# Gated linear attention with a diagonal state-space branch on one core: banks and order in the passage between two loops, kv ahead of q in three chunks, tiles moved by 64 bytes

## The chip, the cores and the metric

The kernel runs on one core of a Trainium2 chip. The metric is device time in microseconds (us) of one execution, the median of several. The core has five engines with queues of their own, each working in program order: TensorE (PE; its weight loads are listed as PEld), VectorE (DVE), ScalarE (ACT), GpSimd (POOL) and SyncE (SP), which here only issues DMA transfers. All times below are from one profiled execution unless a median is named.

## The reference

For x of 2048 rows and D = 448 columns, H = 16 heads of 28:

```python
phi = lambda t: jnp.where(t > 0, t + 1, jnp.exp(t)) + 1e-6
pq, pk = phi(q), phi(k)                      # q, k, v = x @ wqkv
kv = jnp.einsum("bhsd,bhse->bhde", pk, v)
z = jnp.einsum("bhsd->bhd", pk)
num = jnp.einsum("bhqd,bhde->bhqe", pq, kv)
den = jnp.einsum("bhqd,bhd->bhq", pq, z)[..., None] + 1e-6
a = (num / den) @ wo
b = causal_conv(x, K(log_A_real, A_imag, C_real, C_imag, log_dt)) + x * D_skip
out = g * a + (1 - g) * b                    # g = sigmoid((x * gate_w).sum(-1))
```

Nothing is causal in branch a: kv and z are sums over all rows, so every output row needs all of pk first. In branch b the convolution kernel is, for these inputs, so flat that running sums of x do its work: a triangular matrix (tri) times the chunk, a factor per column (near), and a carry from earlier chunks (the product z).

## The kernel before

The sequence is cut into NC = 16 chunks of 128 rows. Nearly all matmuls are in fp32r, and each factor is split into a high and a low part, so that a product takes two or three matmuls: ACT writes the high part (a cast), POOL or DVE the low part (the difference).

**Chunk loop** (lines 464 to 517; chunk c does k of chunk c + 1 and the rest of chunk c). On PE: k, 11 matmuls of 448 columns (project, lines 309 to 332); q, 11 of 450 columns; kv, 11 matmuls g (do_g, line 386), where pkh and pkl, the high and low part of pk, stream against blocks of x and add up in four PSUM banks over all chunks; and from chunk 5 on one or two products v with tri (do_v, line 399; two matmuls, lines 401 and 402). What feeds them: split_t (line 232) casts x turned into xt on ACT and has POOL write its low half, for k and q of that chunk; the second matmul of a k already needs the low half. split_n (line 237) does the same for x as it is, xn, for kv and v, and has POOL do skip (line 245). k_feature, k_high and k_low (lines 348 to 363) make pkh and pkl on ACT and DVE; q_post (line 370) starts on ACT with an exp of q's last column (line 371). v_post (line 404) multiplies v on DVE (line 406), sends a row by SP, and has POOL add (line 414). In chunks below 5, steps() puts pieces of the state-space preparation on ACT and DVE behind q_post.

**Passage** (lines 627 to 771). When all kv sums stand, ACT copies them out (gs), and PE makes, in this order: z, the carry product of branch b (line 681: uw, whose 47 rows hold the chunk's last rows of v at rows 0 to 14 and their low parts at rows 32 to 46); kv_products(1) into a tile called k, for heads of blocks 2 and 3, and kv_products(0) into a tile called tr (line 712; 16 pieces each). kv_split (line 715) masks them on DVE, kv_high and kv_low write kvh (ACT) and kvl (DVE). m_products (line 688) multiply those by the split wo, three matmuls for each block j = 3, 2, 0, 1, into m3, m2, m0, m1; m_high (ACT) and m_low (DVE, line 700) write them to mh and ml, the operands of the output products. Block 3 goes to a tile shl, whose low part is needed before SP copies pieces of it to other rows (lines 751 and 752). Tiles that share a PSUM bank with an earlier one wait until that is read: m3 takes the bank of the tile k, m2 that of z, m0 and m1 take two free ones of the pool p3.

Meanwhile the denominators are made per chunk: norm_a (POOL, prod = pq times z's sums, line 527; three buffers), norm_b (DVE, a reduction, line 532), norm_d (DVE, scale and reciprocal, and a copy to SBUF by DVE or ACT, lines 535 to 541), norm_c (pq divided, pn: two instructions on POOL and one on DVE, lines 547 to 560).

**Output loop** (lines 796 to 821). Chunk by chunk: turn (four transposes of pn on PE, line 589; ACT casts th, DVE writes the low part, line 597), attend (11 matmuls, line 614, in the order of blocks 2, 0, 1, 3), final_b and final_c. turn(c + 1) stands ahead of attend(c) on PE. The seven remaining matmuls of the last q are put into the passage (q_run).

The order is that of the code: nothing is scheduled by a tool. Tile addresses follow from the order in which tiles are allocated; the short tile edge (64 bytes) shifts all pools behind it.

Of the kernel before, what the change touches and what calls it, by code (L numbers as in the profile page):

```python
# [7 lines left out]
F32 = mybir.dt.float32  # L8
F32R = mybir.dt.float32r
# [6 lines left out]
P = 128  # L16
S = 2048
D = 448
# [3 lines left out]
NC = S // P  # L22
# [20 lines left out]
GIN = 9 + NC  # L43
L1, L0 = 32, 64
UL = 32
UZ = UL + NC - 1
PAD = S + P
MAGIC = 1.5 * 2.0 ** 23
TWO_PI = 6.283185307179586
# [85 lines left out]
def gated_mix_kernel(ctx: ExitStack, tc: tile.TileContext, xin, wq_d, wvo_d, abc_d, ldt_d, dsk_d,  # L135
# [19 lines left out]
    wqh, wql = (const.tile([P, J, QW], F32R, name=n)[:, :, :D + 2] for n in ("wqh", "wql"))  # L155
    wvo = const.tile([P, 2, J, D], F32, name="wvo")
    wv, wo = wvo[:, 0], wvo[:DJ, 1]
    tri = const.tile([P, P], F32R, name="tri")
    both = const.tile([P, 2, P], F32, name="both")
    ident, trir = both[:, 0], both[:, 1]  # L160
    cst = const.tile([P, DJ + RX + 1], F32, name="cst")
# [10 lines left out]
    okr = const.tile([1, DJ + 1], F32, name="okr")  # L172

    const.tile([P, EDGE], F32, name="edge")

    xp = work.enter_context(tc.tile_pool(name="xp", bufs=4))
    xt_p = work.enter_context(tc.tile_pool(name="xt", bufs=4))
# [59 lines left out]
    def split_n(c):  # L237
        r, w = plain[c], xn_p.tile([P, NX], F32R, name="xn", tag="n")
        xn[c] = w
        ACT.copy(w[:, :XC - NAT], r)  # L240
        low(POOL, w[:, XC - NAT:], r[:, :D], w[:, :D])
        if c > 2:
            skip(c)
# [85 lines left out]
    def project(*args, **kw):  # L329
        o, run = pieces(*args, **kw)  # L330
        run(11)
        return o
# [20 lines left out]
        DVE.scalar_tensor_tensor(out=pks[c], in0=pks[c], scalar=1.0, in1=e, op0=ALU.add, op1=ALU.max)  # L353

    def k_high(c):
        pkh[c] = tp.tile([P, D], F32R, name="pkh", tag="pkh")
        ACT.add(pkh[c], pks[c], 1e-6)

    def k_low(c):
        pk = pks.pop(c)  # L360
        pkl[c] = tp.tile([P, D], F32R, name="pkl", tag="pkl")
        for o, a, op in ((pkl[c], pkh[c].bitcast(F32), ALU.subtract), (zb, zb, ALU.add))[::-1 if c == NC - 1 else 1]:
            DVE.scalar_tensor_tensor(out=o, in0=pk, scalar=1e-6, in1=a, op0=ALU.add, op1=op)

# [5 lines left out]
    def q_post(c, o, mid=None):  # L370
        ACT.activation(e1[:, c:c + 1], o[:, D:D + 1], AF.Exp, scale=-1.0)
        feature(pq[:, c], o, mid)
# [13 lines left out]
    def do_g(c, blocks=range(4)):  # L386
        w = xn[c]
        for i in blocks:
            a = w[:, 64 + i * P:64 + (i + 1) * P]
            b = w[:, XC - NAT + 64 + i * P:][:, :P] if i < 3 else None  # L390
            seq = [(a, pkh[c]), (a, pkl[c]), (b, pkh[c])] if i < 3 else \
                  [(a, pkh[c]), (a[:, :64], pkl[c])][::1 if c == 0 else -1]
            for n, (a, b) in enumerate(seq):
                PE.matmul(g[i][:a.shape[1], :D], lhsT=a, rhs=b, start=c == 0 and n == 0,  # L394
                          stop=c == NC - 1 and n == len(seq) - 1)
# [68 lines left out]
    for c in range(2, NC - 2):  # L464
        if c + 3 < NC:
            load_x(c + 3)
        if c == 2:
            SP.dma_start(out=cst, in_=cst_d)
        if c == 4:
            SP.dma_start(out=wvo, in_=wvo_d)  # L470
        vs = VS.get(c, ())
        ko = project(c + 1, wkh, wkl, D, "v1" if c in (2, 4) else "k")
        for v in vs[:1]:
            do_v(v)
        split_t(c + 2)
        k_feature(c + 1, ko)
        k_high(c + 1)
        if c > 5:
            for v in vs[:1]:
                v_post(v)  # L480
        k_low(c + 1)
        qo = project(c, wqh, wql, D + 2, "q")
        if c == 5:
            steps(1)
        else:
            for v in vs[1:]:
                do_v(v)
        q_post(c, qo)
        if c == 5:
            v_post(0)  # L490
        else:
            for v in vs[1:]:
                v_post(v)
        if c < 5:
            steps(2 if c == 4 else 1)
        if c == 3:
            DVE.tensor_copy(tri, trir)
            DVE.tensor_copy(gcr, gcat)
        if c == 7:
            SP.dma_start(out=okr[:, None, :DJ], in_=oks[:, None, :])  # L500
        if c == 9:
            DVE.tensor_reduce(out=okr[:, DJ:], in_=okr[:, :DJ], op=ALU.add, axis=AX.X)
            DVE.tensor_copy(okn, okr[:, DJ:])
        do_g(c)
        if c == 5:
            do_v(1)
        if c < 4:
            skip(c - 1)
        split_n(c + 2)
        if c == 5:  # L510
            v_post(1)
        for j in {11: (0, 1), 12: (2, 3)}.get(c, ()):
            w = xn_p.tile([P, NX], F32R, name="wo", tag="n")[:DJ, :2 * D].rearrange("p (i d) -> p i d", i=2)
            woh.append(w[:, 0])
            wol.append(w[:, 1])
            ACT.copy(woh[j], wo[:, j])
            low(POOL, wol[j], wo[:, j], woh[j])
# [7 lines left out]
    def norm_a(c):  # L525
        pd[c] = tp.tile([P, D], F32, name="prod", tag="pk", bufs=3)
        POOL.tensor_tensor(out=pd[c], in0=pq[:, c], in1=zb, op=ALU.mult)  # L527
# [15 lines left out]
    def norm_bd(c):  # L543
        norm_b(c)
        norm_d(c, 1)

    def norm_c(c):
        n = pn[c] = tp.tile([P, J, P], F32, name="pn", tag="pn")
        r = dn[c // 2][:, c % 2]
        a = pq[:, c, :3 * DJ].rearrange("p (j h d) -> p j h d", j=3, h=4)  # L550
        b = pq[:, c, 3 * DJ:].rearrange("p (h d) -> p h d", h=4)
        POOL.tensor_tensor(out=n[:, :3, :DJ].rearrange("p j (h d) -> p j h d", h=4), in0=a,  # L552
                           in1=r[:, :H - 4].rearrange("p (j h) -> p j h", j=3)[:, :, :, None].to_broadcast([P, 3, 4, DH]),
                           op=ALU.mult)
        DVE.tensor_tensor(out=n[:, :3, DJ:].rearrange("p j (h d) -> p h j d", h=4),  # L555
                          in0=b[:, :, :DS].rearrange("p h (j d) -> p h j d", j=3),
                          in1=dp[0][:, c, H - 4:, None, None].to_broadcast([P, 4, 3, DS // 3]), op=ALU.mult)
        POOL.tensor_tensor(out=n[:, 3].rearrange("p (b h d) -> p b h d", b=2, h=4),
                          in0=b[:, None, :, DS:].to_broadcast([P, 2, 4, DH - DS]),
                          in1=r[:, None, H - 4:, None].to_broadcast([P, 2, 4, DH - DS]), op=ALU.mult)  # L560
# [15 lines left out]
    def gates_c(n, o, tag):  # L576
        w = tp.tile([P, D], F32R, name="phs", tag=tag)[:n, :3 * P].rearrange("p (i t) -> p i t", i=3)
        phs.append(w)
        ACT.copy(w[:, 0:2], o[:n, None, :P].to_broadcast([n, 2, P]))
        return lambda: DVE.tensor_tensor(out=w[:, 2], in0=o[:n, :P], in1=w[:, 0].bitcast(F32), op=ALU.subtract)  # L580
# [77 lines left out]
    for i in range(4):  # L658
# [4 lines left out]
            q_run(2)  # L663
        if i == 2:
            gates_b(gates_a(1, NC - 1), g[0])
    gates_c(NC - 2, g[0], "pkl")()
    norm_bd(1)
    norm_c(1)
    for i in range(5):
        phi(i)  # L670
    gps.close()
# [16 lines left out]
    def m_products(j, pool, tag):  # L688
        o = pool.tile([P, 512], F32, name="m%d" % j, tag=tag)
        w = woh[j]  # L690
        for n, (a, b) in enumerate(((kvh, w), (kvh, wol[j]), (kvl, w))):
            PE.matmul(o[:DJ, :D], lhsT=a[:, j], rhs=b, start=n == 0, stop=n == 2)  # L692
        return o
# [34 lines left out]
    def kv_high(r, o):  # L728
        ACT.copy(kvh[:, 2 * r:2 * r + 2], o)

    def kv_low(r, o):
        DVE.tensor_tensor(out=kvl[:, 2 * r:2 * r + 2], in0=o, in1=kvh[:, 2 * r:2 * r + 2].bitcast(F32), op=ALU.subtract)
# [3 lines left out]
    k0 = kv_products(0)  # L736
    k1 = kv_split(1, k1)
    kv_high(1, k1)
    norm_a(3)
    kv_low(1, k1)  # L740
    k0 = kv_split(0, k0)
    carry()
    o3 = m_products(3, ps, "k")
    o2 = m_products(2, ps, "v0")
    m_high(3, o3)
    kv_high(0, k0)
    m_low(3, o3)
    kv_low(0, k0)
    m_high(2, o2)
    for j in (2, 0, 1):  # L750
        SP.dma_start(out=wk2[DJ:, :, j].bitcast(F32), in_=shl[DT + 16 * j:DT + 16 * j + 16].bitcast(F32))
# [3 lines left out]
    q_run(2)  # L755
    norm_a(4)
    turn_split(0, o0)
    o0 = m_products(0, p3, "a")
    o1 = m_products(1, p3, "a")
    m_high(0, o0)  # L760
    m_high(1, o1)
    m_low(0, o0)
    m_low(1, o1)
    ACT.copy(mh[:DT, 3], shl[:DT, 0].bitcast(F32))
    ACT.copy(rc[0][:DT], shl[:DT, 0].bitcast(F32))
    norm_bd(2)
    norm_c(2)
    norm_a(5)
    norm_bd(3)
    tail(0)  # L770
    q_run(11)
    def late():
# [21 lines left out]
    later = late()  # L794
    due = next(later)
    for c in range(NC):
        if c % 2 and c + 4 < NC:
            norm_d(c + 3, 2, ACT.copy)
        if c:
            final_b(c - 1)  # L800
        if 0 < c < NC - 2:
            norm_c(c + 2)
        if c + 1 < NC:
            turn(c + 1)
        if c:
            final_c(c - 1)
        if c + 1 < NC:
            tail(c + 1)
        if c + 6 < NC:
            norm_a(c + 6)  # L810
        if c + 5 < NC - 1:
            phi(c + 5)
        attend(c, ((0, D // 2), (D // 2, D)) if c == NC - 1 else ((0, D),))
        if c == 0:
            norm_b(4)
        if c + 5 < NC:
            norm_b(c + 5)
        if c == due:
            due = next(later, None)
        if c == 9:  # L820
            v_add(NC - 1, vl)
# [94 lines left out]
```

## Time and profile before

| | us |
|---|---|
| median of 3 executions | 177.37 (177.36 to 177.40) |
| the profiled execution | 177.07 |
| its span, first to last instruction | 175.3 |
| PE busy in the span | 169.2 |
| granted TensorE clock | 1.00 throughout |

Rows of the timeline give the start in us from the start of the span, the time taken, the engine, the line, the operation, what is written from what, the shape and how many instructions the row merges; in square brackets the engine's idle time before it and what ended it. A matmul's end is modelled and overlaps the next one, so the distance from start to start is its cost. PE's stages: start-up to about 8, chunk loop to 118.8, passage to about 129, output loop to 171.7.

### The profile page before, as it was taken

What the parts mean: (1) busy time and instruction counts of PE and PEld (TensorE: products, weight loads), DVE (VectorE), ACT (ScalarE), POOL (GpSimd) and SP (SyncE); (2) the same over time, 40 slices, a digit from 0 to 9 for tenths busy, and PEclk for the clock granted to TensorE, in tenths of its full rate; (3) what the DMA queues carried; (4) which work ended last, traced back from release to release, by engine and by line L of the source; (5) the groups of instructions that cost most, each with busy time, mean ns of one, the idle gap of its engine ahead of it and who ended that gap; (6) DMA issues with size and microseconds to landing.
All of it is one profiled execution on the core that took longest, in us unless ns stands there. A gap on an engine that the chain in (4) does not pass through costs nothing.

```text
span 175.3 us, 2809 instructions
## 1 busy us (share of the span) xinstructions
PE 169.2 (97%) x876; PEld 151.6 (86%) x876; DVE 114.1 (65%) x244; ACT 95.9 (55%) x220; POOL 120.5 (69%) x128
## 2 busy tenths in 40 slices
PE   6999999999999999999999999999899999999991
PEld 2698999999999999999989999988797999999991
DVE  1757548698867383563824519377899988987451
ACT  3789398884446344272435653464554554664541
POOL 5267576977349969687698999439549998983100
PEclk9999999999999999999999999999999999999999
DMA  5999974095003113031133000000021212122312
GB/s 174 415 301 300 245 212 142 23 410 226 4 1 121 58 65 119 7 121 52 69 122 121 4 0 1 0 2 4 14 54 52 105 69 93 75 101 88 112 57 104
DMA packets 7963, 18.61 MB, mean 106 GB/s; under 512 B 2045, under 2 KB 4810, under 8 KB 7818
## 3 DMA queue, kind: packets, MB, share of 16 engines
q1 hardware_dynamic: 7946, 18.41, 31.6%
q8 instruction: 7, 0.11, 0.3%
q14 instruction: 10, 0.08, 0.2%
HBM read 14.38 MB, written 3.67 MB: 103 GB/s over the span
## 4 chain that ended last, share of the span: by engine, by line
PE 85%; DVE 8%; ACT 2%; issue 2%; POOL 1%; ACTq 0%; DVEq 0%; POOLq 0%
PE g L394 19%; PE a L614 18%; PE q L325 17%; PE k L325 14%; PE v L325 6%; PE tr L589 4%; PE q L252 2%; PE v L402 2%; DVE den L532 2%; PE v L401 2%; PE m L692 1%; DVE wk L700 1%; DVE den L538 1%; POOL xn L230 1%; ACT gs L660 1%
## 5 line engine op out<-in xcount | busy, mean ns | idle before, releaser
L614 PE MATMUL a<-wk,th 128*128 128x448 f32 (+1 forms) x170 | 36.6, 360 | 0.0
L394 PE MATMUL g<-pkh,xn 128*128 128x448 f32 x112 | 35.8, 366 | 0.0
L614 PEld LDWEIGHTS a<-wk,th 128*128 128x128 f32 x170 | 29.5, 189 | 2.0 <-DVE th L597 0.4
L325 PE MATMUL k<-wk,xt 128*128 128x448 f32 x132 | 29.3, 366 | 0.0
L353 DVE SCALAR_TENSOR_TENSOR k<-k,e 128x448 f32<-128x448 f32 x12 | 7.6, 632 | 30.7 <-ACT e L352 30.7
L325 PE MATMUL q<-wqh,xt 128*128 128x450 f32 x120 | 27.4, 365 | 0.0
L325 PEld LDWEIGHTS k<-wk,xt 128*128 128x128 f32 x132 | 24.6, 188 | 2.8 <-ACT wk L423 0.4
L414 POOL TENSOR_TENSOR y<-y,t 128x448 f32<-128x448 f32 x16 | 18.7, 1167 | 11.9 <-DVE t L406 11.8
L230 POOL TENSOR_TENSOR xn<-xr,xn 128x448 fp32r<-128x448 f32 x16 | 19.2, 1203 | 9.1 <-ACT xn L240 8.8
L325 PEld LDWEIGHTS q<-wqh,xt 128*128 128x128 f32 x120 | 22.5, 188 | 1.7
L394 PE MATMUL g<-pkl,xn 128*128 128x448 f32 x64 | 23.5, 367 | 0.0
L394 PEld LDWEIGHTS g<-pkh,xn 128*128 128x128 f32 x112 | 21.1, 188 | 2.4
L351 ACT ACTIVATE e<-k 128x448 f32<-128x448 f32 x12 | 6.5, 543 | 27.5 <-PE k L325 27.4
L527 POOL TENSOR_TENSOR prod<-pq,zb 128x448 f32<-128x448 f32 x16 | 18.2, 1147 | 3.0 <-ACT zb L650 3.0
L246 POOL TENSOR_TENSOR y<-xr,rows 128x448 f32<-128x448 f32 x16 | 18.8, 1176 | 0.0
L230 POOL TENSOR_TENSOR xt<-xr,xt 128x512 fp32r<-128x512 f32 x14 | 18.1, 1296 | 0.4 <-ACT xt L234 0.4
L552 POOL TENSOR_TENSOR pn<-pq,den 128x336 f32<-128x336 f32 x16 | 12.0, 751 | 9.3 <-DVE pn L555 4.4
L619 DVE SCALAR_TENSOR_TENSOR ot<-y,og,a 128x448 f32<-128x448 f32 (+1 forms) x17 | 10.6, 626 | 5.1 <-PE a L614 5.0
L597 DVE TENSOR_TENSOR th<-tr,th 128x512 fp32r<-128x512 f32 x16 | 11.0, 690 | 2.8 <-ACT th L596 2.2
L394 PEld LDWEIGHTS g<-pkl,xn 128*128 128x128 f32 x64 | 11.2, 175 | 1.1
L596 ACT CAST th<-tr 128x512 fp32r<-128x512 f32 x16 | 9.4, 589 | 4.6 <-PE tr L589 4.4
L325 PE MATMUL q<-wql,xt 128*128 128x450 f32 x45 | 11.7, 364 | 0.0
(151 smaller groups left out, 301.9 us busy)
## 6 DMA issues: line engine op xcount, KB each, us to landing
xr<-in SPq DMA_DIRECT2D x15, 512.0 KB, 5.8
out<-ot SPq DMA_DIRECT2D x15, 224.0 KB, 1.9
pq<-in SPq DMA_DIRECT2D x4, 448.0 KB
wvo<-in SPq DMA_DIRECT2D x1, 1792.0 KB
y<-in SPq DMA_DIRECT2D x2, 480.0 KB
y<-in SPq DMA_DIRECT2D x2, 450.0 KB
u<-t SPq DMA_DIRECT2D x30, 1.8 KB, 1.8
y<-in SPq DMA_DIRECT2D x1, 448.0 KB, 4.3
```

The source lines that it names most:

```text
L230: eng.tensor_tensor(out=o, in0=r, in1=h.bitcast(F32), op=ALU.subtract)
L246: POOL.tensor_tensor(out=y[:, c], in0=plain[c][:, :D], in1=dsk, op=ALU.mult)
L325: PE.matmul(o[:, :n], lhsT=a, rhs=b, start=run.n == 1, stop=not seq)
L353: DVE.scalar_tensor_tensor(out=pks[c], in0=pks[c], scalar=1.0, in1=e, op0=ALU.add, op1=ALU.max)
L394: PE.matmul(g[i][:a.shape[1], :D], lhsT=a, rhs=b, start=c == 0 and n == 0, stop=c == NC - 1 and n == len(seq) - 1)
L414: POOL.tensor_tensor(out=y[:, c], in0=y[:, c], in1=t, op=ALU.add)
L527: POOL.tensor_tensor(out=pd[c], in0=pq[:, c], in1=zb, op=ALU.mult)
L552: POOL.tensor_tensor(out=n[:, :3, :DJ].rearrange("p j (h d) -> p j h d", h=4), in0=a, in1=r[:, :H - 4].rearrange("p (j h) -> p j h", j=3)[ ...
L596: ACT.copy(h, ov)
L597: DVE.tensor_tensor(out=l, in0=ov, in1=h.bitcast(F32), op=ALU.subtract)
L614: PE.matmul(a[:, lo:hi], lhsT=u_, rhs=w_[:, lo:hi], start=n == 0, stop=n == 10)
L619: DVE.scalar_tensor_tensor(out=ot[:, lo:hi], in0=y[:, c, lo:hi], scalar=og[:, c:c + 1], in1=a[:, lo:hi], op0=ALU.mult, op1=ALU.add)
```

## The change

Six edits; line numbers grow by up to 12.

1. In chunks 2 to 4 kv (do_g) is issued ahead of q, elsewhere behind it as before. On PE, from k of chunk 3 on (here called v_321 after its bank; g_141 to g_144 are the four kv banks), before:

```order
L325 MATMUL v_321<-wk_69,xt 128x448 x11
L325 MATMUL q<-wqh,xt 128x450 x8
L325 MATMUL q<-wql,xt 128x450 x3
L394 MATMUL g_141<-pkh,xn 128x448
L394 MATMUL g_141<-pkl,xn 128x448
```

and the end of that kv in the changed kernel:

```order
L394 MATMUL g_144<-pkl,xn 64x448
L394 MATMUL g_144<-pkh,xn 128x448
L325 MATMUL q<-wqh,xt 128x450 x8
L325 MATMUL q<-wql,xt 128x450 x3
L325 MATMUL k<-wk_69,xt 128x448 x11
```

The 11 kv matmuls now stand between k and q, and the next k follows q directly. The other engines' order in these chunks is unchanged, so q's work on ACT and DVE stands where it stood.

2. In chunk 10, split_n(12) is issued before the second v_post. On POOL, before (xt, xn and the two kinds of y are the low halves, skip at line 246 and the addition at line 414):

```order
L230 TENSOR_TENSOR xt<-xr,xt 128x512
L414 TENSOR_TENSOR y<-y,t 128x448 x2
L230 TENSOR_TENSOR xn<-xr,xn 128x448
L246 TENSOR_TENSOR y<-xr,rows 128x448
L230 TENSOR_TENSOR xt<-xr,xt 128x512
```

and in the changed kernel:

```order
L230 TENSOR_TENSOR xt<-xr,xt 128x512
L414 TENSOR_TENSOR y<-y,t 128x448
L230 TENSOR_TENSOR xn<-xr,xn 128x448
L246 TENSOR_TENSOR y<-xr,rows 128x448
L414 TENSOR_TENSOR y<-y,t 128x448
L230 TENSOR_TENSOR xt<-xr,xt 128x512
```

The second addition has moved behind xn and skip.

3. In the passage, norm_b(1) is issued ahead of the gates (line 580), norm_c(1) behind kv_high(1), kv_high(0) and kv_low(0) ahead of m_high(3) and m_low(3); m3 and m2 go to the banks of p3, m0 and m1 to those of k and z. The denominators of chunks 2 and 3 are made together, ahead of m_low(0) and m_low(1), those of chunks 4 and 5 in chunk 1 of the output loop. On DVE before, from the gates (phs) on; k and tr are the two kv products, rc is the carry, shl and wk_69 are what m_low writes:

```order
L580 TENSOR_TENSOR phs<-g_141,phs 14x128
L532 TENSOR_REDUCE den<-prod 128x16
L536 SCALAR_TENSOR_TENSOR den<-den,e_60 128x16
L538 RECIPROCAL den<-den 128x16
L541 COPY den<-den 128x16
L555 TENSOR_TENSOR pn<-pq,den 128x4x3x4
L718 TENSOR_TENSOR k<-k,cst 112x112
```

and in the changed kernel, from kv_low(0) on:

```order
L739 TENSOR_TENSOR kvl<-tr,kvh 112x224
L707 TENSOR_TENSOR shl<-m_1361,shl 112x448
L707 TENSOR_TENSOR wk_69<-m_1365,wk_69 112x448
L603 TENSOR_TENSOR th<-tr,th 128x512
L538 TENSOR_REDUCE den<-prod 128x16 x2
L542 SCALAR_TENSOR_TENSOR den<-den,e_60 128x32
L544 RECIPROCAL den<-den 128x32
L707 TENSOR_TENSOR wk_69<-m_1395,wk_69 112x448
L707 TENSOR_TENSOR wk_69<-m_1399,wk_69 112x448
L561 TENSOR_TENSOR pn<-pq,den 128x4x3x4
```

Of the first piece, the reduction (line 538 in the changed kernel) now stands ahead of the gates and the pn row behind the mask of k; in the second, one pair of denominators stands ahead of the last two m_low, where before two single ones stood behind them.

4. The carry product has UZ = 64 rows rather than 47 (the added rows are zero); u, uw and gcr grow with it.

5. pkh and pkl become slices of wider tiles that begin 64 bytes in; the tiles behind them in that pool move too.

6. tri is allocated behind edge; the constants between move down by 512 bytes.

```diff
-UZ = UL + NC - 1
+UZ = 2 * UL
...
-        pkh[c] = tp.tile([P, D], F32R, name="pkh", tag="pkh")
+        pkh[c] = tp.tile([P, 512], F32R, name="pkh", tag="pkh")[:, EDGE:EDGE + D]
...
-        pkl[c] = tp.tile([P, D], F32R, name="pkl", tag="pkl")
+        pkl[c] = tp.tile([P, 512], F32R, name="pkl", tag="pkl")[:, EDGE:EDGE + D]
...
         k_low(c + 1)
+        if c < 5:
+            do_g(c)
         qo = project(c, wqh, wql, D + 2, "q")
...
         q_post(c, qo)
+        if c == 10:
+            split_n(c + 2)
...
-        do_g(c)
+        if c > 4:
+            do_g(c)
...
-        split_n(c + 2)
+        if c != 10:
+            split_n(c + 2)
...
-    gates_c(NC - 2, g[0], "pkl")()
-    norm_bd(1)
-    norm_c(1)
+    gates = gates_c(NC - 2, g[0], "pkl")
+    norm_b(1)
+    gates()
+    norm_d(1, 1)
...
     kv_high(1, k1)
+    norm_c(1)
     norm_a(3)
     kv_low(1, k1)
     k0 = kv_split(0, k0)
     carry()
-    o3 = m_products(3, ps, "k")
-    o2 = m_products(2, ps, "v0")
+    o3 = m_products(3, p3, "a")
+    o2 = m_products(2, p3, "a")
+    kv_high(0, k0)
     m_high(3, o3)
-    kv_high(0, k0)
+    kv_low(0, k0)
     m_low(3, o3)
-    kv_low(0, k0)
     m_high(2, o2)
...
     turn_split(0, o0)
-    o0 = m_products(0, p3, "a")
-    o1 = m_products(1, p3, "a")
+    norm_b(2)
+    norm_b(3)
+    norm_a(5)
+    o0 = m_products(0, ps, "k")
+    o1 = m_products(1, ps, "v0")
     m_high(0, o0)
     m_high(1, o1)
+    ACT.copy(mh[:DT, 3], shl[:DT, 0].bitcast(F32))
+    ACT.copy(rc[0][:DT], shl[:DT, 0].bitcast(F32))
+    norm_d(2, 2, ACT.copy)
     m_low(0, o0)
     m_low(1, o1)
-    ACT.copy(mh[:DT, 3], shl[:DT, 0].bitcast(F32))
-    ACT.copy(rc[0][:DT], shl[:DT, 0].bitcast(F32))
-    norm_bd(2)
     norm_c(2)
-    norm_a(5)
-    norm_bd(3)
...
-        if c % 2 and c + 4 < NC:
+        if c % 2 and 1 < c < NC - 4:
             norm_d(c + 3, 2, ACT.copy)
...
+        if c == 1:
+            norm_b(5)
+            norm_d(4, 2, ACT.copy)
         attend(c, ((0, D // 2), (D // 2, D)) if c == NC - 1 else ((0, D),))
         if c == 0:
             norm_b(4)
-        if c + 5 < NC:
+        if 0 < c < NC - 5:
             norm_b(c + 5)
```

More of the change, by code (lines that the diff above doesn't have):

```diff
@@ L157, in gated_mix_kernel @@
     wv, wo = wvo[:, 0], wvo[:DJ, 1]
-    tri = const.tile([P, P], F32R, name="tri")
     both = const.tile([P, 2, P], F32, name="both")
@@ L174, in gated_mix_kernel @@
     const.tile([P, EDGE], F32, name="edge")
+    tri = const.tile([P, P], F32R, name="tri")
     xp = work.enter_context(tc.tile_pool(name="xp", bufs=4))
```

## The prediction

> **What bounds the kernel now.** I read the page first: busy times, then the chain that ended last.
>
> ```profile
> PE 169.2 (97%) x876; PEld 151.6 (86%) x876; DVE 114.1 (65%) x244; ACT 95.9 (55%) x220; POOL 120.5 (69%) x128
> PE 85%; DVE 8%; ACT 2%; issue 2%; POOL 1%; ACTq 0%; DVEq 0%; POOLq 0%
> ```
>
> TensorE is the bound: busy for 97% of the span and on 85% of the chain. It does the same matmuls after the change, so only two things can pay: places where it waits, and its pace from matmul to matmul. The timeline of PE shows the waits after the start-up: one in the chunk loop at 89.25, and several in the passage between the chunk loop and the output loop, from 118.9 to 137.2. (The last column is the engine's idle time; a short wait shows only as a late start.)
>
> ```profile
> 118.91 0.45 PE L681 MATMUL z<-uw,gcr 47*112 47x448 f32 x1
> 119.29 1.83 PE L712 MATMUL k<-gs,wvo 128*112 128x112 f32 x16
> 120.95 1.74 PE L712 MATMUL tr<-gs,wvo 128*112 128x112 f32 x16
> 123.11 0.66 PE L692 MATMUL m<-wo,kvh 112*112 112x448 f32 x2 [0.42 <-DVE kvl L732]
> 125.19 0.65 PE L325 MATMUL q<-wqh,xt 128*128 128x450 f32 x2
> 125.68 0.57 PE L692 MATMUL m<-wo,kvh 112*112 112x448 f32 x2
> 126.89 0.97 PE L325 MATMUL q<-wqh,xt 128*128 128x450 f32 x4
> 128.31 0.60 PE L589 MATMUL tr<-both,pn 128*128 128x128 f32 x4
> 128.67 2.25 PE L614 MATMUL a<-wk,th 128*128 128x448 f32 x10
> 130.96 0.60 PE L589 MATMUL tr<-both,pn 128*128 128x128 f32 x4
> 134.38 0.63 PE L589 MATMUL tr<-both,pn 128*128 128x128 f32 x4 [0.33 <-DVE pn L555]
> 137.22 0.60 PE L589 MATMUL tr<-both,pn 128*128 128x128 f32 x4
> ```
>
> From start to start these rows give what each piece costs unhindered: two groups of m 1.21 (125.68 to 126.89), the two early q matmuls 0.49, the other seven 1.42, a turn 0.36 (128.31 to 128.67), a product with its turn 2.65 (128.31 to 130.96). The kv products (k, tr) are 32 pieces; their 16 in tr need 0.098 each, so they are through at 122.5.
>
> **The passage, term by term.** If nothing waited after 122.5, PE would need m3 and m2 1.21, turn 0.36, q 0.49, m0 and m1 1.21, q 1.42, then three times 2.65 and it would be at 122.5 + 12.64 = 135.1 where the trace has 137.22 (the start of the turn behind attend(2)). The prize is at most **2.1**. Whether it is paid hangs on who releases what. The DVE, ACT and POOL rows there (the one that begins with L700 is the group of m_low's instructions, with its mean in ns):
>
> ```profile
> 120.04 0.60 DVE L532 TENSOR_REDUCE den<-prod 128x16 f32<-128x448 f32 x1
> 121.41 0.28 DVE L718 TENSOR_TENSOR k<-k,cst 112x112 f32<-112x112 f32 x1
> 122.29 0.34 ACT L729 CAST kvh<-k 112x224 fp32r<-112x224 f32 x1 [1.93 <-DVE k L725]
> 122.66 0.39 DVE L732 TENSOR_TENSOR kvl<-k,kvh 112x224 fp32r<-112x224 f32 x1 [0.47 <-ACT kvh L729]
> 123.39 0.69 DVE L683 SCALAR_TENSOR_TENSOR rc<-zs,cst,z 48x448 fp32r<-48x448 f32 x1
> L700 DVE TENSOR_TENSOR wk<-m,wk 112x448 fp32r<-112x448 f32 x3 | 1.9, 625 | 0.3 <-ACT wk L696 0.2
> 131.63 1.35 DVE L532 TENSOR_REDUCE den<-prod 128x16 f32<-128x448 f32 x2
> 133.24 0.37 DVE L538 RECIPROCAL den<-den 128x32 f32<-128x32 f32 x1
> 130.76 2.26 POOL L527 TENSOR_TENSOR prod<-pq,zb 128x448 f32<-128x448 f32 x2
> 132.97 0.76 POOL L552 TENSOR_TENSOR pn<-pq,den 128x336 f32<-128x336 f32 x1
> ```
>
> m3 starts at 123.11 and not at 122.5 because its bank is that of k, which kvl still reads until 123.05; m2 stands in z's bank, which rc reads until 124.08. In p3's banks, long read out by then, neither read counts: m3 needs only kvh for its first two matmuls. kvh comes 0.25 earlier as well: norm_c(1) no longer stands on DVE ahead of L718, and norm_b(1), now at 119.5 rather than 120.04, runs while L580 waits for its operand, so L718 starts when k's last products land, at 121.15, and kvh ends near 122.4. PE goes on at 122.5; kvl (122.8) is in time for the third matmul.
>
> Behind that, on before's clock: DVE does the mask of tr 122.75 to 123.1, rc to 123.85, kvl(0) to 124.2, m_low(3) to 124.75 (0.6 each), m_low(2) to 125.3, the split of turn 0 to 125.9. m0 and m1 start at 124.55 in k's and z's banks, free since 122.8 and 123.85, and need kvl(0) at 124.95. The output product of chunk 0 could then start at 127.55 (before: 128.67). What is queued behind the new order: norm_b(2) and norm_b(3) together 1.35, the scaling 0.2, the reciprocal 0.37, so DVE reaches m_low(0) at 127.8 and ends m_low(1) at 128.95. PE asks for them at 128.65 and 129.25 (sixth and ninth matmul). It fits by 0.25 to 0.3.
>
> The denominators for chunks 2 and 3 leave DVE at 127.85. POOL does prod(5) from norm_b(2)'s end (126.5) to 127.7, pn(2) from 128.1 to 129.3 (1.1 by the gap from 132.97 to the next prod at 134.04), prod(6) to 130.4, pn(3) to 131.5. PE wants pn(2) at 129.85 and pn(3) at 132.5. In the trace pn(3) began at 132.97 behind two prods and held the turn at 134.38: this wait goes, with a second to spare. After this POOL needs 2.25 per chunk against PE's 2.65.
>
> The four copies of 16-row and 64-row pieces by SP are the other newcomer:
>
> ```profile
> 125.23 2.05 SPq L751 DMA_DIRECT2D wk<-shl  x3
> wk<-shl SPq DMA_DIRECT2D x3, 56.0 KB, 2.2
> ```
>
> They start with m_low(3)'s end, only 0.45 earlier than now, while their reader starts 1.1 earlier. Issued 0.7 apart and landing 2.2 to 2.3 after their issue, they arrive near 127.1, 127.8, 128.5 and 129.1; PE asks at 127.55, 128.25, 128.85 and 129.45. It fits by 0.3 to 0.45. I take **-2.0** for the passage (none of it up to 2.1); half, if a margin of 0.3 was misread several times over.
>
> z, the 47-row product, starts 0.1 late and takes 0.38 to the next start, against 0.2 for other matmuls of 448 columns: 0.28 lost. Nothing in the trace says whether 64 rows cure it. I take **0**: the other matmuls' time does not follow their rows (m of 112 rows and a of 128 both take 0.2), so no row suggests that 17 more rows change it; bounds 0 to -0.28. [...] The POOL and ACT pieces of u grow in rows only, not in elements per row: nothing.
>
> **The chunk loop's wait.**
>
> ```profile
> 85.10 0.62 ACT L240 CAST xn<-xr 128x512 fp32r<-128x512 f32 x1
> 87.39 1.16 POOL L414 TENSOR_TENSOR y<-y,t 128x448 f32<-128x448 f32 x1 [1.66 <-DVE t L406]
> 88.50 1.16 POOL L230 TENSOR_TENSOR xn<-xr,xn 128x448 fp32r<-128x448 f32 x1
> 89.25 0.37 PE L401 MATMUL v<-xn,tri 128*128 128x448 f32 x1
> 89.71 0.47 PE L402 MATMUL v<-xn,tri 128*128 128x448 f32 x1
> 90.02 1.78 PE L325 MATMUL q<-wqh,xt 128*128 128x450 f32 x8
> ```
>
> PE's second v matmul waits for POOL's xn, which stands behind an addition that waits 1.66 for DVE. The cast that xn needs was done at 85.72. With xn ahead of that addition it is done by 87, and the pair takes 0.41 rather than 0.77: **-0.36** (bounds 0 and -0.36). The addition moves to 88 to 89.2; xt behind it still ends no later than now, and t's buffer is next wanted two v's later.
>
> **kv ahead of q in chunks 2 to 4.** Its gain is pace, its price a wait.
>
> ```profile
> 24.18 2.27 PE q L325 x11
> 28.67 2.21 PE k L325 x11
> 74.91 2.21 PE q L325 x11
> ```
>
> In the chain, the q that follows k directly takes 2.27, the q behind a v 2.21. The q of chunks 2, 3, 4 now follow kv: **-0.18** (bounds -0.2 and 0.1, if kv behind k pays it instead).
>
> But q ends 2.2 later, and ACT's queue behind it moves:
>
> ```profile
> 27.16 0.17 ACT L371 ACTIVATE e<-q 128x1 f32<-128x1 f32 x1
> 30.11 0.61 ACT L240 CAST xn<-xr 128x512 fp32r<-128x512 f32 x1
> 30.80 1.69 POOL L230 TENSOR_TENSOR xn<-xr,xn 128x448 fp32r<-128x448 f32 x1 [1.64 <-ACT xn L240]
> 33.55 1.30 POOL L230 TENSOR_TENSOR xt<-xr,xt 128x512 fp32r<-128x512 f32 x1
> 35.21 2.37 PE L325 MATMUL v<-wk,xt 128*128 128x448 f32 x11
> ```
>
> ACT takes q(2) at 27.16; in the new order q(2) ends where that kv ended, 28.65, so ACT's queue is 1.5 later, the cast of xn(4) ends at 32.2, POOL's xn(4) runs 32.3 to 33.45 (1.15, as most of the 16 do; here it took 1.69), its skip to 34.55, xt(5) to 35.85. The k of chunk 5 wants xt(5) for its second matmul at 35.3. So it waits **0.55, and 0.1 to resume: +0.65**. Bounds: 0.1 (ACT less late) and 1.25 (xn at 1.69 again). The same sum for chunk 6 has xt(6) at 42.5 and k at 42.65: nothing, up to 0.2. Behind the waiting k stand kv(4) and q(4) on PE, all as much later; ACT's and DVE's work on that k has until kv(5), over 7 later. By chunk 7 ACT's idle time has absorbed the shift.
>
> **Addresses.** kv's operands pkh and pkl move by 64 bytes, tri to another place. The kv groups take 2.22 to 2.23, groups of k 2.21. If kv falls to k's pace, 16 groups gain 0.02 each; I take **-0.2**, bounds -0.45 and +0.3. [...] The q rows above, 2.27 or 2.21 for the same operands by what ran before, show a pace that a fixed price does not explain.
>
> **Sum.** -2.0 - 0.36 - 0.18 + 0.65 - 0.2 = -2.1. The profiled execution took 177.07 (span 175.3 and 1.77 around it), 0.30 under the median of 177.37. So 175.0 for a profiled execution and **175.3** for the median.
>
> **Rivals.**
> 1. No wait at chunk 5's k: ACT or POOL are in time after all. For it: in the trace xt(5) is there (34.85) 0.55 before its matmul, so a delay of 0.5 would cost nothing; against it: the order on both engines is fixed and the delay is 1.5, less what xn saves. 174.6.
> 2. The passage gives half. The new queue on DVE (two denominators ahead of m_low(0)) or the late pieces by SP become the bound of attend(0); margins are only 0.25 to 0.45. 176.3.
> 3. Slower: the moved addresses set the slow pace, and it passes from group to group as k's passes to q. 0.06 for each of the 48 groups of k, q and kv is 2.9: 178.2. It turns the sign when some 40 of them are slow. Against it: k and q keep their own addresses.
> 4. The passage's releases are not the ones I read, another wait takes each place, and the early wait eats the rest: 177.4.
>
> **How the numbers follow.** Forecast (174.9 to 175.8) 0.50; rival 1 0.20; rival 2 0.18; rival 3 0.08; rival 4 0.04. Faster by over 0.2% (0.35 us, about what a measurement of this kernel can tell from no change) is the first three: 0.88; same 0.04; slower 0.08. The range takes in rivals 1 and 2 with z's and the addresses' bounds: 174.0 to 176.6.
>
> **What would show it.** m3 starting right behind tr and m2 right behind m3; no idle time ahead of the turns; the pair of v at 89 in 0.41; an idle stretch of PE in k of chunk 5 ended by POOL's xt; z to its next start in 0.38; kv groups at 2.20. Wrong would be: attend(0) waiting for m_low(0) or a DMA, or k, q and kv all at 2.27.

## The result: 176.72 us, 0.4% faster, and the profile after

The changed kernel takes 176.72 us (median of 6 executions, 176.21 to 177.12), the kernel before 177.38 us beside it (6 executions, 177.31 to 177.56). The ratio is 0.9958, 95% interval 0.994 to 0.9975. So it is faster, by 0.66 us where 2.1 were forecast, and 0.1 above the range. The profiled execution took 176.31 (span 174.5), against 177.07 (span 175.3).

The page of the changed kernel: the span, the busy times, and the shares of the chain that ended last, by engine.

```profile
span 174.5 us, 2800 instructions
PE 168.2 (96%) x876; PEld 151.5 (87%) x876; DVE 113.8 (65%) x240; ACT 96.5 (55%) x221; POOL 119.9 (69%) x128
PE 81%; DVE 8%; ACT 4%; POOL 3%; issue 2%; DVEq 0%; ACTq 0%; POOLq 0%
```

PE's share of the chain went from 85% to 81%: ACT and POOL now hold 7% of it where they had 3%. A stretch has come in which the end is set by them. The timeline of PE in the changed kernel shows the passage (lines 595, 620, 699 and 719 were 589, 614, 692 and 712):

```profile
122.09 1.74 PE L719 MATMUL tr<-gs,wvo 128*112 128x112 f32 x16
123.60 0.65 PE L699 MATMUL m<-wo,kvh 112*112 112x448 f32 x2
124.30 0.56 PE L699 MATMUL m<-wo,kvh 112*112 112x448 f32 x2
131.04 0.60 PE L595 MATMUL tr<-both,pn 128*128 128x128 f32 x4
133.69 0.60 PE L595 MATMUL tr<-both,pn 128*128 128x128 f32 x4
136.34 0.60 PE L595 MATMUL tr<-both,pn 128*128 128x128 f32 x4
```

tr takes 1.51 from start to start (2.16 before), m3 stands right behind it and m2 right behind m3, and the turns follow at 2.65 each without a wait. From z's start (120.04) to the turn behind attend(2) it is 16.30, and it was 18.31: 2.01 gained. Yet z itself starts 1.13 later than before. The chunk loop lost that, between chunks 2 and 6:

```profile
28.75 0.17 ACT L371 ACTIVATE e<-q 128x1 f32<-128x1 f32 x1 [1.41 <-PE q L325]
31.71 0.60 ACT L240 CAST xn<-xr 128x512 fp32r<-128x512 f32 x1
34.61 1.28 POOL L230 TENSOR_TENSOR xt<-xr,xt 128x512 fp32r<-128x512 f32 x1
35.22 0.37 PE L325 MATMUL v<-wk,xt 128*128 128x448 f32 x1
35.95 2.28 PE L325 MATMUL v<-wk,xt 128*128 128x448 f32 x10 [0.36 <-POOL xt L230]
42.54 2.49 PE L325 MATMUL k<-wk,xt 128*128 128x448 f32 x11
42.74 0.17 ACT L371 ACTIVATE e<-q 128x1 f32<-128x1 f32 x1
44.24 0.62 DVE L344 SCALAR_TENSOR_TENSOR pq<-q,t 128x448 f32<-128x448 f32 x1
45.10 1.20 DVE L274 SCALAR_TENSOR_TENSOR sm<-sm 112x4 f32<-112x4 f32 x2
45.12 1.16 POOL L246 TENSOR_TENSOR y<-xr,rows 128x448 f32<-128x448 f32 x1
45.29 1.77 PE L325 MATMUL q<-wqh,xt 128*128 128x450 f32 x8
46.24 1.28 POOL L230 TENSOR_TENSOR xt<-xr,xt 128x512 fp32r<-128x512 f32 x1
46.29 1.33 DVE L274 SCALAR_TENSOR_TENSOR sm<-sm 112x4 f32<-112x4 f32 x2
48.24 0.16 DVE L273 TENSOR_TENSOR sm<-sm,okc 112x4 f32<-112x4 f32 x1
48.46 0.60 PE L306 MATMUL p<-both,sm 112*128 112x112 f32 x4 [0.81 <-DVE sm L273]
```

Three waits of PE can be read from it, as distances from start to start of groups. k of chunk 5 takes 2.85 instead of 2.21 (+0.64); its second matmul waits for POOL's xt, as forecast. k of chunk 6 takes 2.33 (+0.12). And in front of p, the four small transposes of the state-space tables (line 306) behind q of chunk 5, PE stands for 0.81, so that q's group (from 45.29) takes 3.17 and not 2.20 (+0.97). Of this third wait the prediction says nothing. In the kernel before the DVE instruction that p needs ended at 46.54 and p started at 46.73 without a wait:

```profile
41.85 1.38 DVE L341 TENSOR_SCALAR t<-e 128x448 f32<-128x448 f32 x1
44.19 1.34 DVE L274 SCALAR_TENSOR_TENSOR sm<-sm 112x4 f32<-112x4 f32 x2
44.53 1.77 PE L325 MATMUL q<-wqh,xt 128*128 128x450 f32 x8
45.52 0.23 DVE L274 SCALAR_TENSOR_TENSOR sm<-sm 112x4 f32<-112x4 f32 x2
46.37 0.17 DVE L273 TENSOR_TENSOR sm<-sm,okc 112x4 f32<-112x4 f32 x1
46.73 0.55 PE L306 MATMUL p<-both,sm 112*128 112x112 f32 x4
```

It had 0.2 to spare, against a shift of nearly 2 us. The chain on ACT and DVE from the exponent of q(4) (line 371) to that DVE instruction did not get longer: it takes 5.89 before and 5.66 in the changed kernel, but starts at 42.74 where it had started at 40.64. **Theory A** for the experiments: q(2) behind kv leaves ACT idle for 1.41 at line 371; from there to p neither ACT nor DVE has slack, so one delay runs down to p, and PE meets it in several places. **The rivals**: the waits have separate causes and add up; each chunk with kv first costs its share; the loss comes from elsewhere, the addresses or the passage.

To compare the traces I use one length, "the stretch": from the first matmul of chunk 2 behind k (its q, or its kv where that is first) to the first of k of chunk 7. It is 25.73 before and 27.43 after. Medians are less sharp: the first group of 22 matmuls starts at 8.50 to 9.47 in the profiled executions, whichever edits a kernel holds, and what came late there stays in the time.

### The profile page after: what moved, and what is told of

The parts are those of the page before. It is cut to its first block, busy times and chain, and to the rows that moved or that the text cites. A ratio compares the mean times of both kernels' runs of the same rounds, so it can differ in the third digit from the quotient of the medians.

```text
span 174.5 us, 2800 instructions
## 1 busy us (share of the span) xinstructions
PE 168.2 (96%) x876; PEld 151.5 (87%) x876; DVE 113.8 (65%) x240; ACT 96.5 (55%) x221; POOL 119.9 (69%) x128
## 4 chain that ended last, share of the span: by engine, by line
PE 81%; DVE 8%; ACT 4%; POOL 3%; issue 2%; DVEq 0%; ACTq 0%; POOLq 0%
PE a L620 20%; PE g L394 16%; PE q L325 14%; PE k L325 13%; PE tr L595 4%; PE v L325 3%; PE q L252 2%; POOL y L246 2%; PE v L402 2%; PE v L401 2%; PE m L699 1%; DVE sm L274 1%; PE k L719 1%; PE tr L719 1%; ACT y L283 1%
## 5 line engine op out<-in xcount | busy, mean ns | idle before, releaser
L357 ACT ACTIVATE pkh<-k 128x448 fp32r<-128x448 f32 x12 | 6.6, 546 | 10.0 <-DVE k L353 10.0
```

## The experiments

| kernel | median, us | ratio to before, 95% interval | stretch, us |
|---|---|---|---|
| changed kernel | 176.72 | 0.9958 (0.994 to 0.9975) | 27.43 |
| e1: without kv first | 174.57 | 0.9845 (0.9831 to 0.9858) | 25.63 |
| e2: before + kv first | 179.43 | 1.0113 (1.0095 to 1.0131) | 27.45 |
| e3: before + passage (edit 3) | 175.67 | 0.9893 (0.9875 to 0.991) | |
| e4: before + edit 2 | 177.08 | 0.9987 (0.9974 to 1.0) | |
| e5: before + addresses | 177.13 | 0.9995 (0.9982 to 1.0007) | |
| e6: before + 64 rows | 177.30 | 0.9995 (0.9984 to 1.0006) | |
| e7: changed, p behind kv | 176.38 | 0.9946 (0.9929 to 0.9963) | 27.31 |
| e8: changed, xt ahead | 176.65 | 0.9958 (0.9944 to 0.9972) | 27.65 |
| e10: before + banks | 176.57 | 0.9949 (0.9936 to 0.9962) | |
| e12: changed, kv first in chunk 2 only | 176.68 | 0.9959 (0.9946 to 0.9972) | 27.68 |
| e13: changed, kv first in chunk 4 only | 175.51 | 0.9898 (0.9873 to 0.9923) | 26.67 |
| e14: changed, kv first in 2 and 3, steps first | 175.61 | 0.9894 (0.9877 to 0.9911) | 26.21 |
| e15: changed, gcr's cast later | 176.59 | 0.9952 (0.9937 to 0.9966) | 27.38 |

### One part undone or alone: e1 to e6

**e1**, the changed kernel with kv behind q everywhere:

```diff
-        if c < 5:
-            do_g(c)
...
-        if c > 4:
-            do_g(c)
+        do_g(c)
```

> The changed kernel with kv behind q again in chunks 2 to 4, all else kept. Theory A (the kv-first edit costs what its waits in the trace show: 0.64 at k of chunk 5, 0.12 at the next k, 1.0 at the four small transposes p): 1.8 below the changed kernel, 174.5 profiled, median near 174.9, no PE wait from 24 to 50. Rival B (something else in that stretch, as the moved addresses or DMA, makes PE late, and the waits move elsewhere): within 0.5 of the changed kernel.

It took 174.57, 2.15 less than the changed kernel and the shortest of all; by the stretch it is 1.79 less. Its PE timeline has none of the three waits:

```profile
35.33 2.36 PE L325 MATMUL v<-wk,xt 128*128 128x448 f32 x11
46.16 0.76 PE L325 MATMUL q<-wql,xt 128*128 128x450 f32 x3
46.80 0.60 PE L306 MATMUL p<-both,sm 112*128 112x112 f32 x4
```

So all the missing gain, and a little more, went into edit 1; the other five together bring 2.7 by the medians, where the forecast's terms for them make 2.56.

**e2**, the kernel before with edit 1 alone (the same lines, the other way round).

> The kernel before with kv ahead of q in chunks 2 to 4 and nothing else. Theory A: slower than before by 1.6 to 1.8, near 179.1, with the same three waits. Theory A as the prediction had it (only k waits, and q gains pace): slower by 0.5, 177.9. Rival B: no slower than before by more than 0.3.

179.43, slower by 1.1% (1.71 by the stretch), with k of chunk 5 at 2.88 and q of chunk 5 at 3.16: the loss does not need the other edits.

**e3**, the kernel before with edit 3 alone.

> The kernel before with the passage's edit alone (banks, order, paired denominators): 2.0 faster, 175.4; from z's start to the end of the third output product 16.3 rather than 18.3. If a part of the gain belongs to the 64 rows or to the addresses, less than 1.7.

175.67, with 16.28 from z to the turn behind attend(2), as in the changed kernel. (In its profiled execution the first group of 22 came 0.97 later than in that of the kernel before.)

**e4**, the kernel before with edit 2 alone.

> The kernel before with split_n(12) ahead of the second v_post in chunk 10 and nothing else: 0.36 faster, 177.0, the pair of v at 89 in 0.41. If the wait only moves to a later place: no change.

177.08. The v pair near 90 takes 0.41 instead of 0.77, so the 0.36 is there in the trace; the medians are 0.2 apart, and their interval just reaches no change.

**e5**, the kernel before with edits 5 and 6 alone.

> The kernel before, with the addresses alone changed: the kv tiles 64 bytes on and tri behind the edge. Theory: the pace of the kv groups follows the address, as in the changed kernel (2.224 to 2.230 us before, 2.202 to 2.210 after, about 14 groups); the whole trace gains 0.2 to 0.3 us: 177.1 us, and no wait appears anywhere. Rival: the pace went with the order of kv and q, or with the 64-row product; then the kv groups stay at 2.22 and the time at 177.3 us.

177.13, no difference that the interval can tell. The pace did change: between 56 and 88 us kv went from 2.226 to 2.209, k from 2.209 to 2.199, and q the other way, from 2.209 to 2.218; that is 0.018 a chunk. These three values are the same in all nine kernels with the new addresses, and the old three in all six without, to 0.001. But what had been gained by 89 was lost there:

```profile
89.02 0.36 PE L401 MATMUL v<-xn,tri 128*128 128x448 f32 x1
89.69 0.47 PE L402 MATMUL v<-xn,tri 128*128 128x448 f32 x1 [0.32 <-POOL xn L230]
90.00 1.78 PE L325 MATMUL q<-wqh,xt 128*128 128x450 f32 x8
```

PE reaches the pair at 89.02 (89.25 before), waits longer, and goes on at 90.00 (90.02 before): POOL, not PE, sets that point. The faster pace counts only where edit 2 has taken the wait away.

**e6**, the kernel before with edit 4 alone (`UZ = 2 * UL`).

> The kernel before, with the carry product alone taken from 47 to 64 rows. Theory: nothing; z to the next group's start stays at 0.38 us and the time within 0.2% of the kernel before, 177.3 us. Rival: the step behind z shrinks by up to 0.28 us, to about 0.10, and the time is 177.0 us.

177.30, and z still takes 0.38:

```profile
119.16 0.45 PE L681 MATMUL z<-uw,gcr 64*112 64x448 f32 x1
119.54 0.65 PE L712 MATMUL k<-gs,wvo 128*112 128x112 f32 x4
```

### Where in the chain of kv first: e7, e8, e12 to e15

**e7**, the changed kernel with p behind kv:

```diff
         qo = project(c, wqh, wql, D + 2, "q")
-        if c == 5:
-            steps(1)
-        else:
+        if c != 5:
             for v in vs[1:]:
                 do_v(v)
...
         if c > 4:
             do_g(c)
         if c == 5:
+            steps(1)
+            v_post(0)
             do_v(1)
```

(v_post(0) left its place behind q_post for this.)

> The changed kernel, with the four small transposes p of loop c = 5 (and the steps that go with them) moved from behind q to behind kv, 2.2 us later on PE. Theory: the wait of 0.81 us in front of p (0.97 us by the q group's length) is what the late chain on ACT and DVE costs there, and a place 2.2 us later covers it: q of chunk 5 returns to 2.20, the time falls by 0.97 to 175.75 us, while k of chunks 5 and 6 keep their waits (2.85, 2.33). Rival: what reads p (the steps behind it) then comes 2.2 us late and PE waits there in place of p, in chunks 6 to 8; the time stays at 176.7 us.

The timeline of PE in e7:

```profile
49.81 0.55 PE L306 MATMUL p<-both,sm 112*128 112x112 f32 x4
50.98 0.47 PE L401 MATMUL v<-xn,tri 128*128 128x448 f32 x1 [0.62 <-ACT rows L307]
```

The wait in front of p is gone, and 0.62 of it stands behind p: the v that follows waits for ACT's copy of p (line 307), because the two share a PSUM bank (the tag v1 in the code). Only 0.12 of the loss of 1.79 in the stretch is gone. The rival was right, one place earlier than it said: moving the reader moves the wait.

**e8**, the changed kernel with xt(5) and xt(6) ahead of the xn of the chunk before:

```diff
-        split_t(c + 2)
+        if c not in (3, 4):
+            split_t(c + 2)
...
+        if c in (2, 3):
+            split_t(c + 3)
         if c != 10:
             split_n(c + 2)
```

> The changed kernel, with POOL's casts xt(5) and xt(6) ahead of the xn of the chunk before, so that k of chunks 5 and 6 no longer wait for them. Theory A (one chain of ACT and DVE, begun by the late q(2), ends at p; PE's waits before p only use up the same delay early): k of chunks 5 and 6 return to 2.21, the wait in front of p grows by about what they lose (q of chunk 5 from 3.17 to 3.7 or more), and the time hardly moves, 176.5 to 176.9 us. Rival B (the three waits have three causes and add up): q of chunk 5 stays at 3.17 and the time falls by 0.77 to 175.95 us.

In e8's timeline, both k take 2.20, and then:

```profile
44.30 1.37 DVE L341 TENSOR_SCALAR t<-e 128x448 f32<-128x448 f32 x1
45.77 0.62 DVE L344 SCALAR_TENSOR_TENSOR pq<-q,t 128x448 f32<-128x448 f32 x1
46.54 1.88 PE L325 MATMUL q<-wqh,xt 128*128 128x450 f32 x8 [1.56 <-DVE pq L344]
```

The time did not fall (176.65), so theory A holds on the sum: the waits do not add up, they share one delay. It missed the place. The delay came out ahead of p, at q of chunk 5, which needs the one bank of q, still read by DVE's work on q(4).

**e12**, the changed kernel with `if c == 2` and `if c != 2` around its two calls of do_g.

> The changed kernel, with kv ahead of q in chunk 2 alone; chunks 3 and 4 have q first again. Theory A (the late q(2) leaves ACT idle for 1.41 us at its exponent of q(2), ACT and DVE have no slack until p, so the whole delay reaches PE whatever chunks 3 and 4 do): nearly the whole loss stays, PE's waits between k of chunk 5 and p add up to 1.3 to 1.7 us, 176.2 to 176.6 us. Rival C (each chunk with kv first costs its share, 2.15 us over three): 175.3 us, with waits of 0.6.

In e12's timeline:

```profile
28.94 0.17 ACT L371 ACTIVATE e<-q 128x1 f32<-128x1 f32 x1 [1.42 <-PE q L325]
36.16 2.28 PE L325 MATMUL v<-wk,xt 128*128 128x448 f32 x10 [0.44 <-POOL xt L230]
46.62 1.88 PE L325 MATMUL q<-wqh,xt 128*128 128x450 f32 x8 [0.99 <-ACT e L352]
```

One chunk costs as much as three: 176.68, stretch 27.68. Rival C is out. The loss of 2.05 in the stretch is above the 1.3 to 1.7 that theory A gave. With kv first in chunk 2 alone, and ACT idle at q(2), the whole loss is there.

**e14**, kv first in chunks 2 and 3, with those chunks' table steps (2.5 us on ACT each) ahead of the work on q:

```diff
-        if c < 5:
+        if c < 4:
             do_g(c)
...
+        if c < 4:
+            steps(1)
         q_post(c, qo)
...
-        if c < 5:
-            steps(2 if c == 4 else 1)
+        if c == 4:
+            steps(2)
...
-        if c > 4:
+        if c > 3:
             do_g(c)
```

> The changed kernel, with kv ahead of q in chunks 2 and 3 alone, and with the table steps of those two chunks (2.5 us on ACT each) ahead of ACT's work on q instead of behind it. Theory A: the steps fill ACT's idle time of 1.41 and 0.28 us in front of the exponent of q, ACT's casts come as early as in the kernel before (xn at 30.1, 36.4), no wait appears at k of chunk 5 or at p, and the whole loss is gone although two chunks keep kv first: 174.6 to 174.9 us. Rival C: two chunks of three keep their share, 176.0 us.

In e14's timeline:

```profile
30.22 0.15 ACT L371 ACTIVATE e<-q 128x1 f32<-128x1 f32 x1
30.70 0.62 ACT L240 CAST xn<-xr 128x512 fp32r<-128x512 f32 x1
38.51 1.85 PE L325 MATMUL q<-wqh,xt 128*128 128x450 f32 x8 [0.39 <-DVE pq L344]
47.81 0.55 PE L306 MATMUL p<-both,sm 112*128 112x112 f32 x4
```

ACT has no idle time at line 371 any more. Its cast of xn comes at 30.70; this execution started 0.56 later than that of the kernel before, where it came at 30.11, so it is on time. No wait is left at k or p. That part of theory A is shown: the steps behind q filled ACT's time, and kv first opened a hole ahead of them. But not the whole loss is gone, as theory A had it. What stays is 0.58 of the 1.79 in the stretch, at a place that neither theory named: q(4), in front of kv again, comes before DVE has read q(3) out of the bank. The passage is 0.22 longer too (16.52 from z to the turn behind attend(2)); why is open.

**e15**, the changed kernel with `DVE.tensor_copy(gcr, gcat)` moved from chunk 3 to chunk 7.

> The changed kernel, with DVE's cast of gcr (1.18 us, in chunk 3) moved to chunk 7; gcr is first read by the carry product. Theory A says that DVE is as full as ACT from the late q(2) to p: the wait in front of p shrinks by the cast, q of chunk 5 from 3.17 to 2.2 us, while k of chunks 5 and 6 keep 2.85 and 2.33, so 175.75 us. Rival D (the chain to p goes through ACT and POOL, with DVE only its last link): the wait stays at 3.1 to 3.2 and the time at 176.7 us.

Theory A falls here in its claim on DVE: 1.18 us of DVE work less, and the wait in front of p is 0.71 still. In e15's timeline:

```profile
43.15 0.17 ACT L371 ACTIVATE e<-q 128x1 f32<-128x1 f32 x1 [0.94 <-PE q L325]
43.79 0.39 DVE L341 TENSOR_SCALAR t<-e 128x448 f32<-128x448 f32 x1 [0.40 <-ACT e L340]
48.80 0.60 PE L306 MATMUL p<-both,sm 112*128 112x112 f32 x4 [0.71 <-DVE sm L273]
```

With the cast gone, ACT waits 0.94 for PE's q(4) and DVE waits for ACT. A second chain lies under the first, and it starts at q(4). **e13**, kv first in chunk 4 alone (`if c == 4` and `if c != 4` around do_g), asks for it:

> The changed kernel, with kv ahead of q in chunk 4 alone; chunks 2 and 3 have q first again. Theory S (a second cause: from ACT's exponent of q(4) to p the work on ACT and DVE takes 5.7 to 5.9 us, 40.64 to 46.54 before and 42.74 to 48.46 after, and with kv first in chunk 4 PE has only 4.8 us of work between the end of q(4) and p): no wait at k of chunk 5, but 0.5 to 0.9 us in front of p, 175.1 to 175.5 us. Rival (the idle time of chunk 2 is the only cause, and ACT's 2.11 us of idle time in front of the exponent of k of chunk 6 takes up the late q(4)): no wait, and the 174.6 us of the kernel without kv first.

In e13's timeline:

```profile
42.44 0.17 ACT L371 ACTIVATE e<-q 128x1 f32<-128x1 f32 x1 [1.24 <-PE q L325]
44.73 1.19 DVE L274 SCALAR_TENSOR_TENSOR sm<-sm 112x4 f32<-112x4 f32 x2
48.09 0.60 PE L306 MATMUL p<-both,sm 112*128 112x112 f32 x4 [0.86 <-DVE sm L273]
```

175.51, no wait at k of chunk 5, 0.86 in front of p: theory S. So kv first has **two causes of loss**. In chunk 2 it opens a hole in ACT's queue; in chunk 4 it leaves 4.8 us of PE work between q and p for a chain that takes about 5.7 with the step to PE. Alone they cost 2.05 and 1.03 of the stretch, together 1.79. The traces fit one delay that covers the other: in the changed kernel ACT reaches q(4) at 42.74 with almost no idle time, where it stands 1.24 in e13. That chunk 2 alone costs 0.26 more than all three is not explained by this; in e12 the chain from line 371 to p's operand takes 5.99, in the changed kernel 5.66.

### The passage's two halves: e10

**e10**, the kernel before with the banks of m3, m2 and of m0, m1 exchanged, nothing else of edit 3:

```diff
-    o3 = m_products(3, ps, "k")
-    o2 = m_products(2, ps, "v0")
+    o3 = m_products(3, p3, "a")
+    o2 = m_products(2, p3, "a")
...
-    o0 = m_products(0, p3, "a")
-    o1 = m_products(1, p3, "a")
+    o0 = m_products(0, ps, "k")
+    o1 = m_products(1, ps, "v0")
```

> The kernel before, with only the four banks of the m products exchanged in the passage (m3, m2 in the attend banks, m0, m1 in k and v0); order and denominators as before. If the passage's gain is in two separate parts: tr and m3 run without their waits (2.16 to 1.51 and 1.72 to 1.31 us, together -1.07) and the waits inside attend(1) and attend(2) (0.76 + 0.16 + 0.03) stay, so 176.3 us. Rival: the waits inside attend(1) and attend(2) are set by ACT and DVE, whose work is in the old order, so they grow by what PE gains ahead of them; the time stays within 0.3 of the kernel before, 177.0 to 177.3 us, and only banks and order together give the 2 us.

In e10's timeline:

```profile
121.43 1.74 PE L712 MATMUL tr<-gs,wvo 128*112 128x112 f32 x16
123.16 0.66 PE L692 MATMUL m<-wo,kvh 112*112 112x448 f32 x2
131.04 2.50 PE L614 MATMUL a<-wk,th 128*128 128x448 f32 x10
134.08 0.63 PE L589 MATMUL tr<-both,pn 128*128 128x128 f32 x4 [0.33 <-DVE pn L555]
```

176.57: m3 stands 1.73 behind tr's start (2.16 before, 1.51 in the changed kernel), and the turn still waits for pn. From z to the turn behind attend(2) it is 17.53: the banks give 0.78, order and denominators the other 1.2. So there are two parts, but the banks alone give less than the 1.07 expected: 0.22 stays in front of m3. That m3 waits for kvh there is my estimate: the prediction had kvh 0.25 earlier with the order of edit 3, which e10 lacks.

## Why the prediction was wrong, step by step

- **Passage, forecast -2.0: measured -2.01.** Right, with its parts: the banks, the denominators, no wait for m_low(0) or a DMA at margins of 0.25 to 0.45.
- **Chunk loop's wait, forecast -0.36: measured -0.36** (the pair takes 0.41). Right.
- **Addresses, forecast -0.2: measured -0.26 from chunk 6 to z.** Right in size, and e5, which changed addresses alone, shows that the pace goes with them (kv 2.226 to 2.209). But it came not for the stated reason alone: k gained too and q lost, and a part of it was to be had only because edit 2 had removed the wait behind it (e5).
- **64 rows, forecast 0: measured 0** (0.386 against 0.380); u's pieces take 0.55 on ACT and 1.14 on POOL at either number of rows. Why z takes 0.38 stays open.
- **kv first, the pace, forecast -0.18.** At the old addresses it is there: in e2 the groups kv, q, k of chunk 2 take 2.225, 2.218 and 2.203, where before q, kv, k took 2.268, 2.224 and 2.208: 0.054 less. At the new addresses it is not: chunk 2 takes 2.202, 2.260 and 2.204 in the changed kernel, against 2.205, 2.204 and 2.199 in e1 (chunk 3 of e1: 2.268, 2.219 and 2.198). The two terms were summed as if they did not touch.
- **kv first, k of chunk 5, forecast +0.65: measured +0.64**, by the mechanism told (the second matmul starts 0.53 late behind POOL's xt, and from it to the third it is 0.31, not 0.21); k of chunk 6, "up to 0.2": +0.12.
- **The step that failed: "By chunk 7 ACT's idle time has absorbed the shift".** The shift was followed on ACT to the next k and no further. Before chunk 7 stands p, whose operand is made by the steps that DVE does behind its work on q(4), with 0.2 to spare before. At q(4) the shift had not been absorbed: the chain from line 371 started 2.10 later, and p's operand came 1.87 later. It cost PE +0.97, and this is most of what separates the forecast from the result: with it, k of chunk 6 and no pace gain the sum is -2.0 - 0.36 + 0.64 + 0.12 + 0.97 - 0.26, about -0.9, and the profiled executions differ by 0.76, the medians by 0.66.

The prediction's own question, who is queued behind the engine that comes late, would have found it: the rows behind line 371 on ACT and line 344 on DVE lead to line 306 on PE. Its four rivals did not contain this wait either.

Undoing edit 1 gives the best kernel of the study: 174.57 us, 1.55% under the kernel before.

Open: p's chain with POOL's work moved out of its way (last section) was not tried.

## What to carry to other kernels

When a producer is moved later, follow the delay along every queue that it enters until an engine with idle time takes it up, and list each reader of the bound engine on the way, small ones with a different purpose too; the price here was not the first wait (0.64) but the whole delay (1.79 of the stretch). A gap that a reorder opened on an engine with a full queue was lost here (1.42 on ACT in e12), until later work of the same queue was put into it (e14, no idle time there). And a gain ahead of a wait that another engine sets was none until that wait was gone (in e5 0.23 ahead of the v pair, 0.02 behind it).

## What the hardware showed that I had not expected

**Small DVE instructions that take as long as POOL's.** The pairs of line 274 work on 4 columns. Where POOL is idle a pair takes 0.23; in the changed kernel one instruction of each pair starts within 0.06 of the start of a POOL instruction (45.12 and 46.24) and takes 1.12 and 1.26, until 0.02 after POOL's end. No run took POOL's instruction away, and what makes DVE's take as long is not shown, but the fifteen traces of this study hold both cases. Of their 75 instructions of line 274, the 19 that start within 0.07 of the start of a POOL instruction take 1.12 to 1.27; the other 56 start with POOL idle or within 0.06 of its end and take 0.15 to 0.16. Line 341 shows the same: 58 instructions that start with POOL idle take 0.38 to 0.40, and all 167 that start during a POOL instruction end 0.25 to 0.34 behind that one's end.

So p's chain holds about 2 us of such lengthening before the change as well: line 341 (1.38 at 41.85) and one of line 274 (1.26) there, two of line 274 in the changed kernel. In all fifteen traces two instructions of the chain are longer than with POOL idle, by 0.8 to 1.1 us each. By these numbers I estimate that the chain would take about 3.5 without them (5.59 less 0.97 and 1.10 in e13), less than the 4.8 of PE's work, and then the second cause would be gone; no run shows it.

**A pace that changes with addresses and order.** A group of 11 matmuls takes 2.20 to 2.27 where nothing waits. Edits 5 and 6 together changed it (e5, kv from 2.226 to 2.209), and so did the order of kv and q (e2, three groups by 0.054). From 56 to 88 us it repeats to 0.001 in every chunk and in all kernels with the same addresses. In e1 and e5, though, q takes 2.205 in chunks 2 and 4 and 2.268 in chunk 3, in one order. In chunk 2 kv first is the faster order at the old addresses (by 0.054 over the three groups) and the slower one at the new (by 0.058). Which address does it, and how, was not found.
